# Attention and state-space convolution on one core: the normalization's multiplications go from VectorE to GpSimd, and the order is set anew

## The chip, the core and the metric

The kernel runs on one core of one Trainium2 chip. The metric is device time in microseconds (us) of one execution; each kernel is executed several times and the median is compared. The core has TensorE (PE in the profile, its weight loads PEld), VectorE (DVE), ScalarE (ACT), GpSimd (POOL) and SyncE (SP). SP issues most DMA transfers, GpSimd issues some, among them all those that add into their destination.

## The reference

Two independent layers are computed and laid side by side in the output. The second is attention with 32 query heads that share one key and one value head of 18 numbers:

```python
q = (x @ wq).reshape(B, S, H, Dh).transpose(0, 2, 1, 3)      # S = 2048, H = 32, Dh = 18
k = x @ wk;  v = x @ wv
scores = einsum("bhqd,bkd->bhqk", q, k) * (Dh ** -0.5)
o = einsum("bhqk,bkd->bhqd", softmax(scores, axis=-1), v)
b = o.transpose(0, 2, 1, 3).reshape(B, S, H * Dh) @ wo
```

The first is a long convolution of a 2048 x 576 input along its length, with a kernel that is a sum of 128 complex exponentials per channel, computed by transforms:

```python
P = exp(logdA[:, :, None] * l[None, None, :])                # 576 channels, 128 states, 2048 positions
K = einsum("dn,dnl,dn->dl", Cc, P, dB).real
y = irfft(rfft(pad(u)) * rfft(pad(K)))[:, :L] + u * Dskip
```

## The kernel before

Attention works through four chunks c of 512 queries. In a chunk, 16 pairs of heads run over 16 blocks kb of 128 keys; one such step for two heads is a *score step*, and there are 1024. A score step is two half-precision matmuls on TensorE (tile `s`), one exponential on ScalarE over 128x1024 (tile `P`), and the products of `P` with the values, in full precision, summed in PSUM (tile `ops`). The values have a column of ones, so that each head's sum of exponentials comes out as row 18 of its 32 rows. TensorE gets three score steps at a time; between them it does the products and *filler*: the projections of the queries (`q`), bounds for the exponent (`up`), the output projection (`op`), and the matmuls of the convolution (`kg`, `hu`, `lu`, `hk`, `lk`, `iy`).

`gather` (L768) copies the finished `ops` of four heads to SBUF on VectorE (tile `o`) and stores it to DRAM (`od`). When a chunk's eight groups are stored, `normalize` (L777) makes the rows that the output projection reads:

- it loads the sums (`dn`), takes reciprocals on VectorE and stores them (`rden`),
- it loads the unnormalized rows into `oT`, in five parts m of 126 rows (the last has 72),
- for each part it loads the reciprocals of its heads, each repeated over 18 rows (tile `db`, two buffers), and multiplies `oT` by them.

The first three chunks are normalized whole (15 multiplications). The last is done in four pieces as its head groups finish (`LATE`, 4 multiplications), and what its output projection has not reached by the last exponential is done in `finish` (L822), in matmuls called `fin`.

The convolution runs in 12 blocks beside it. VectorE builds tables (`tab`, `tt`), spectra (`ks` of the kernel, `us` of the input) and their products (`acc`, `t`); GpSimd issues the DMAs that add one tile into another: one `ks<-ks` per block, after whose landing the products `acc<-us,ks` may start, and two `acc<-t` with a `t<-t` between them, after whose landing the block is transformed back. GpSimd also issues the stores of the projected queries (`qd`) and of their bounds (`sd`).

One instruction stream per engine is written out by a planner in the kernel's own code. `Clock` keeps an estimated time for each engine and for each piece of memory, and the parts of the kernel are generators (`Stream`, L384) that yield what they wait for: `"p"` for a turn on TensorE, `"v"` for a time on VectorE's clock. The order in which they are resumed by these estimates is the order in which instructions are written into the engines' queues. On the chip each engine takes its queue strictly in that order and waits on semaphores for its inputs. The filler shares one bank of PSUM (`bank`, L479), so its next matmuls wait for VectorE's copy out of that bank.

In `normalize` the multiplication is written into VectorE's queue when the planner's clock says that `db` and `oT` have landed. The constants that the estimates use (`HOP`, `FETCH`, `SLACK`, `OVER`, `BACK`, `WF`) stand at the top of the file.

Of the kernel before, what the change touches and what calls it, by code (L numbers as in the profile page):

```python
# [13 lines left out]
ALU = mybir.AluOpType  # L14
# [39 lines left out]
URGENT = 9.6825  # L54
HELD = 0
PATIENCE = 0
SLACK = 0.1532
FEW = 9
NEW = 3
LET = -0.0566  # L60
PLAN = 0.7938
START = 11.4238
OVER = 0.8933
CLEAR = 1.826

LATE = {1: [0], 3: [1], 5: [2], 6: [3]}
# [10 lines left out]
HALF_PI = 1.5707963  # L77


HOP = 0.0401  # L80
GRAIN = 128
FIRST = 25.4233
FETCH = 4.0451
ROOM = 0.3903
INTO = 0.114
BACK = 0.0861
TIGHT = 0.1942
WF = 6.8815
WI = 0.9251
WK = 0.9218  # L90
WB = 1.4569
EPS = 0.0224


# [10 lines left out]
class Clock:  # L105
# [15 lines left out]
    def reset(self, t, v, a):  # L121
        self.t, self.v, self.a, self.g, self.q, self.fill = t, v, a, a, a, 0.0
        self.mem = {}
        self.lanes = [[], []]
        self.block, self.since = self.n // 256, t - FETCH

    def fetch(self):

        if self.n // 256 != self.block:
            self.t = max(self.t, self.since + FETCH * (self.n // 256 - self.block))  # L130
            self.block, self.since = self.n // 256, self.t
# [54 lines left out]
    def end(self, e, t, out, ins, lag):  # L186
        for x in ins:
            c = self.cells(x)
            if c:
                c[1][c[3]] = np.maximum(c[1][c[3]], t + HOP)  # L190
        c = self.cells(out) if out is not None else None
# [3 lines left out]
    def turn(self, mode):  # L195

        if mode != self.mode:
            self.t += INTO if mode else BACK
            self.mode = mode

    def pe(self, cost, out=None, ins=()):
        self.fetch()
        self.turn(0)
        self.t = self.begin(1, self.t, out, tuple(ins)) + cost
        self.end(1, self.t, out, tuple(ins), 0.166 + HOP)

    def act(self, cost, out=None, ins=(), func=None):
# [3 lines left out]
        self.a = self.begin(2, self.a, out, ins) + cost  # L211
        self.end(2, self.a, out, ins, 0.12 + HOP)
        return self.a

    def dve(self, cost, out, ins):
        self.v = self.begin(3, self.v, out, ins) + cost
        self.end(3, self.v, out, ins, 0.09 + HOP)
        self.work += cost
# [39 lines left out]
    def land(self, r, t, new):  # L258
        old, r[3] = r[3], t
        for c, k, lag in ((r[4], 0, HOP), (r[5], 1, HOP)):  # L260
            if c and t != old:
# [6 lines left out]
    def filled(self):  # L268

        self.fill = self.v + HOP + 0.03  # L270


class Queue:
# [5 lines left out]
    def dma_start(self, out, src, **k):  # L279
        self.k.dma(self.name, out, src, "accum_op" in k)  # L280
        return self.q.dma_start(out, src, **k)  # L281

    def activation(self, out, src, func, **k):
        self.k.act(0.07 + math.prod(out.shape[1:]) / 1.2e3, out, (src,), func)
        return self.q.activation(out, src, func, **k)
# [29 lines left out]
class Vector:  # L315
# [13 lines left out]
    def tensor_tensor(self, out, a, b, **k):  # L329
        self.cost(1.042e-3, out, a, b)  # L330
        return self.v.tensor_tensor(out, a, b, **k)  # L331
# [26 lines left out]
class Stream:  # L358
# [30 lines left out]
    def go(self, step, credit, lock=None):  # L389
# [4 lines left out]
        if self.kind == "p":  # L394
            ready = self.ready if self.holds else max(self.ready, k.fill)
            if credit <= 0 or k.t < ready - EPS or lock not in (None, self):
                return False
        if self.kind == "v" and (max(k.t, k.v) < self.ready - EPS or k.v > k.t + self.ahead):
            return False
# [16 lines left out]
class Attention:  # L416
# [342 lines left out]
    def normalize(self, c, ms):  # L759

        nc, V, K = self.nc, self.V, self.k
        od = self.od[c].rearrange("(h r) n -> h r n", r=32)
        if ms[0] == 0:
            self.oT = self.cp.tile([P, 5, CT], F32, tag="oT", name=f"oT{c}")
        o = self.oT
        h0, h1 = MT[ms[0]][0] // DH, sum(MT[ms[-1]]) // DH
        n = (h1 - h0) * CT // P
        dn = self.p1.tile([P, P], F32, tag="dn", name=f"dn{c}_{h0}")  # L768
        rd = self.dr.tile([H, CT], F32, tag="rden", name=f"rden{c}_{h0}")
        nc.sync.dma_start(dn[:n, :], od[h0:h1, DH, :].rearrange("h (a n) -> h a n", n=P))  # L770
        yield "v", lambda: K.at(dn), False
        V.tensor_scalar(dn[:n, :], dn[:n, :], 1e-37, None, op0=ALU.max)
        V.reciprocal(dn[:n, :], dn[:n, :])
        nc.sync.dma_start(rd[h0:h1, :].rearrange("h (a n) -> (h a) n", n=P), dn[:n, :])
        for m in ms:
            m0, mn = MT[m]
            nc.sync.dma_start(o[:mn, m, :], od[m0 // DH:(m0 + mn) // DH, 0:DH, :])  # L777
        tiles = {}

        def fetch(m):  # L780
            m0, mn = MT[m]
            tiles[m] = self.p1.tile([P, CT], F32, tag="db", name=f"db{c}_{m}", bufs=2)
            nc.sync.dma_start(tiles[m][:mn, :], rd[m0 // DH:(m0 + mn) // DH, :].unsqueeze(1).broadcast_to([mn // DH, DH, CT]))
        for m in ms[:2]:
            fetch(m)
        for m in ms:
            mn = MT[m][1]
            yield "v", lambda: K.at(tiles[m], o[:, m, :]), False
            V.tensor_tensor(o[:mn, m, :], o[:mn, m, :], tiles[m][:mn, :], op=ALU.mult)
            if m + 2 in ms:  # L790
                fetch(m + 2)

# [177 lines left out]
    def main(self, conv, flag):  # L970
# [29 lines left out]
        def beside(left, new):  # L1000
# [3 lines left out]
            if new and self.due < self.step + URGENT:  # L1004
                left += OVER
            elif new and any(st.live and st.kind == "p" and st.ready < K.t + CLEAR for st in conv.streams):
# [34 lines left out]
        def fill(i):  # L1041

            free = max(K.s[(i + j) % NS] - 0.225 * j for j in range(NS)) - 0.113
            late = free + SLACK
            while True:
# [150 lines left out]
class Conv:  # L1196
# [384 lines left out]
    def early(self):  # L1581
# [5 lines left out]
        self.streams = [Stream(g, self.k) for g in (self.fronts(), self.inputs(), self.kernels(), self.backs())]  # L1587
        for st, share in zip(self.streams, (WF, WI, WK, WB)):
            st.share = share
# [188 lines left out]
```

## Time and profile before

| what | value |
|---|---|
| median of 3 runs | 1154.71 us (1153.86 to 1155.09) |
| the profiled execution's own time | 1157.21 us |
| its span on the core | 1155.0 us |
| granted TensorE clock over the span | 0.992 |
| TensorE busy | 1096.4 us, 95% |
| ScalarE busy | 1021.8 us, 88% |
| VectorE busy | 935.8 us, 81% |
| GpSimd busy | 96.4 us, 8%, nearly all of it the issuing of DMAs |

The share of VectorE is a mean: it is higher in most stages and falls when the convolution ends. In the rows below an instruction's line is L281, L296 or L331 where a helper issues it (a DMA, a matmul, VectorE's tensor_tensor), so the tile names tell which one it is. A number in square brackets behind a row of the timeline is the time for which that engine stood idle before it, and what released it. The row "PEclk" is the share of its clock that TensorE was granted.

### The profile page before, as it was taken

Reading aid. Unit: us, or ns where it says so; the run is one execution under the profiler, and the core shown is the slowest. Engines: PE = TensorE matmul, PEld = TensorE weight load, DVE = VectorE, ACT = ScalarE, POOL = GpSimd, SP = SyncE. Lnnn points to the kernel's source line nnn. Section 1 sums busy time; section 2 is a strip of 40 time slices with the busy share of each in tenths; the row PEclk is TensorE's granted clock in tenths of the full one; section 3 lists DMA queues with packets and bytes.
Section 4 is the critical chain, followed back from the end, with each engine's and each line's share of the span. In section 5 each row is a group of like instructions: output and inputs, shape, how many; then the busy total and the mean of one; then the engine's idle time right before and its main releaser. Section 6 shows DMA issues by size and latency. Waiting matters only on the chain. (4 is left out here: it accounts for less than half of the span.)

```text
span 1155.0 us, 42904 instructions
## 1 busy us (share of the span) xinstructions
PE 1096.4 (95%) x18660; PEld 556.4 (48%) x18660; DVE 935.8 (81%) x1910; ACT 1021.8 (88%) x1092; POOL 96.4 (8%) x150
## 2 busy tenths in 40 slices
PE   7999979999998899999999999999989899999997
PEld 2454544445454455544454455545544445555444
DVE  5988964878797898998988998989999887873423
ACT  4998969999996998999999899999999898989993
POOL 1100110121010000001011100000010200001000
PEclk9999989999998999999999999999999999999999
DMA  7322442244233316127144325144261413235211
GB/s 282 130 64 94 113 112 79 77 112 117 93 92 96 113 46 145 39 72 197 45 148 108 87 67 160 33 122 106 77 164 42 138 58 80 82 68 129 83 39 45
DMA packets 55124, 114.19 MB, mean 99 GB/s; under 512 B 7500, under 2 KB 25053, under 8 KB 53651
## 3 DMA queue, kind: packets, MB, share of 16 engines
q1 hardware_dynamic: 43715, 77.88, 20.3%
q0 software_dynamic: 10784, 33.10, 14.0%
q8 instruction: 148, 2.42, 0.9%
q10 hardware_dynamic: 432, 0.43, 0.1%
q14 instruction: 45, 0.37, 0.1%
HBM read 48.60 MB, written 36.60 MB: 74 GB/s over the span
## 5 line engine op out<-in xcount | busy, mean ns | idle before, releaser
L749 ACT ACTIVATE P<-s 128x1024 f32<-128x1024 f32 x992 | 941.3, 1028 | 96.5 <-PE s L296 89.5
L296 PE MATMUL ops<-P,v_sb 128*32 128x256 f32 (+1 forms) x8848 | 551.6, 367 | 9.3 <-DVE o L335 7.1
L296 PEld LDWEIGHTS ops<-P,v_sb 128*32 128x32 f32 x8848 | 267.9, 110 | 212.5 <-issue 72.2
L296 PE MATMUL s<-aug,kaug 55*128 55x512 f16 x2048 | 294.1, 382 | 9.8 <-ACT P L749 7.4
L296 PEld LDWEIGHTS <-kaug 55*128 55x128 f16 x2048 | 95.6, 94 | 192.2 <-issue 144.1
L296 PE MATMUL q<-x,wq_sb 128*32 128x256 f32 x1360 | 86.0, 383 | 3.2 <-DVE un L343 3.2
L296 PE MATMUL op<-wo_sb,oT 126*32 126x288 f32 (+1 forms) x1096 | 79.3, 408 | 2.1 <-DVE out L335 2.1
L331 DVE TENSOR_TENSOR tab<-tab,tt 128x576 f32<-128x576 f32 (+1 forms) x72 | 59.2, 822 | 1.7
L296 PEld LDWEIGHTS q<-x,wq_sb 128*32 128x32 f32 x1360 | 40.7, 110 | 39.2 <-issue 11.0
L331 DVE TENSOR_TENSOR tab<-tab 128x576 f32<-128x576 f32 (+1 forms) x72 | 58.9, 819 | 0.0
L331 DVE TENSOR_TENSOR ks<-ks 128x384 f32<-128x384 f32 (+2 forms) x84 | 55.8, 669 | 1.4
L331 DVE TENSOR_TENSOR t<-us,ks 128x576 f32<-128x576 f32 x72 | 50.4, 753 | 0.0
L296 PEld LDWEIGHTS op<-wo_sb,oT 126*32 126x32 f32 (+1 forms) x1096 | 33.1, 110 | 31.4 <-issue 6.2
L331 DVE TENSOR_TENSOR acc<-acc 128x768 f32<-128x768 f32 (+1 forms) x48 | 40.5, 855 | 8.1 <-DMA acc<-t 7.5
L281 POOL DMA_DIRECT2D qd<-qh x46 | 25.9, 596 | 220.1 <-DVE qh L339 214.7
L296 PE MATMUL kg<-tab 128*32 128x64 f32 x2304 | 42.3, 220 | 1.6 <-DVE ksb L335 0.4
L296 PEld LDWEIGHTS kg<-tab 128*32 128x32 f32 x2304 | 36.2, 110 | 14.5 <-issue 4.8
L281 POOL DMA_DIRECT2D acc<-t x24 | 20.7, 863 | 254.9 <-PE s L296 66.0
L331 DVE TENSOR_TENSOR us<-us 128x384 f32<-128x384 f32 (+1 forms) x60 | 37.1, 634 | 1.0
L331 DVE TENSOR_TENSOR acc<-us,ks 128x768 f32<-128x768 f32 x36 | 32.6, 953 | 4.6 <-DMA ks<-ks 4.6
L331 DVE TENSOR_TENSOR us<-lu,scu 128x384 f32<-128x384 f32 x48 | 24.4, 550 | 14.3 <-PE lu L296 14.3
L747 ACT ACTIVATE P<-s,nb 128x1024 f32<-128x1024 f32 x32 | 32.9, 1117 | 2.5 <-PE s L296 2.4
(457 smaller groups left out, 1052.5 us busy)
## 6 DMA issues: line engine op xcount, KB each, us to landing
acc<-t POOLq DMA_DIRECT2D x12, 864.0 KB, 7.5
od<-o SPq DMA_DIRECT2D x31, 256.0 KB
park<-two SPq DMA_DIRECT2D x6, 1152.0 KB
acc<-t POOLq DMA_DIRECT2D x12, 576.0 KB, 5.7
aug<-qd SPq DMA_DIRECT2D x124, 54.0 KB
u<-u SPq DMA_DIRECT2D x12, 384.0 KB
kd<-ksb SPq DMA_DIRECT2D x12, 384.0 KB
kt<-kd SPq DMA_DIRECT2D x48, 96.0 KB
```

The source lines that it names most:

```text
L281: return self.q.dma_start(out, src, **k)
L296: return self.e.matmul(out, w, x, **k)
L331: return self.v.tensor_tensor(out, a, b, **k)
L747: nc.scalar.activation(pt, ps, AF.Exp, scale=SCALE / UNIT ** 2, bias=self.nb)
L749: nc.scalar.activation(pt, ps, AF.Exp, scale=SCALE / UNIT ** 2)
```

## The change

The multiplication of `oT` by `db` is issued to GpSimd. It is written into GpSimd's queue right behind the loads of its operands, before the planner's clock has them landed; the planner then books 1.3 us for it on GpSimd's clock (`POOLED`) and resumes the generator when the product should be there. Seven constants of the planner change as well, so the order of all engines' queues is written anew. Arithmetic, tiles and DMA transfers are the same.

```diff
-SLACK = 0.1532
+SLACK = 0.1682
-OVER = 0.8933
+OVER = 0.8763
-HOP = 0.0401
+HOP = 0.0421
-FETCH = 4.0451
+FETCH = 2.983
-BACK = 0.0861
+BACK = 0.0872
-WF = 6.8815
+WF = 6.9146
+POOLED = 1.3
...
+    def tensor_tensor(self, out, a, b, **k):
+        return self.q.tensor_tensor(out, a, b, **k)
...
         for m in ms:
             mn = MT[m][1]
-            yield "v", lambda: K.at(tiles[m], o[:, m, :]), False
-            V.tensor_tensor(o[:mn, m, :], o[:mn, m, :], tiles[m][:mn, :], op=ALU.mult)
+            K.g = K.begin(4, K.g, o[:, m, :], (o[:, m, :], tiles[m])) + POOLED
+            K.end(4, K.g, o[:, m, :], (o[:, m, :], tiles[m]), 0.15)
+            nc.gpsimd.tensor_tensor(o[:mn, m, :], o[:mn, m, :], tiles[m][:mn, :], op=ALU.mult)
+            yield "v", lambda: K.at(o[:, m, :]), False
             if m + 2 in ms:
                 fetch(m + 2)
```

All queues are word for word the same up to score step 129 of 1024; behind it they differ throughout. TensorE has the same work: 36 of its 256-column products are split into two of 128 columns, and 12 matmuls of the last chunk's output projection are named `fin` instead of `op`, which is the third place below.

VectorE, normalization of the first chunk, where it copies a finished `ops` to SBUF (`o_0`). Before:

```order
533 L331 TENSOR_TENSOR tab_1_4911<-sum_4502,r__4418 128x24x32
534 L331 TENSOR_TENSOR tab_1_4911<-r__4418,dif_4503 128x24x32
535 L331 TENSOR_TENSOR tt_1_8_0_5123<-f__4196,sum_4502 128x768
536 L331 TENSOR_TENSOR oT_4679<-oT_4679,db_2_5002 126x512
537 L331 TENSOR_TENSOR oT_4679<-oT_4679,db_3_5024 126x512
538 L335 COPY o_0_5158<-ops_0_4684 128x512
```

and now:

```order
537 L335 TENSOR_TENSOR tab_1_4899<-tab_1_4899 128x24x24
538 L335 TENSOR_TENSOR tab_1_4899<-tab_1_4899,tt_1_8_4_5103 128x24x24
539 L335 TENSOR_TENSOR acc_5176<-us_3756,ks_4522 128x4x4x48 x2
540 L343 TENSOR_SCALAR qh_1_5100<-q_1_0_5141 128x256
541 L355 SCALAR_TENSOR_TENSOR ql_1_5101<-q_1_0_5141,qh_1_5100 128x256
542 L339 COPY o_0_5206<-ops_0_4684 128x512
```

The copy stood behind two multiplications that wait for `db`; now it stands behind products `acc<-us,ks`, whose operand `ks` is completed by a DMA from GpSimd's queue.

GpSimd, the same place. Before:

```order
45 L281 DMA ks_4454<-ks_4454 128x768
46 L281 DMA acc_4947<-t_4948 128x1728
47 L281 DMA qd_5018<-qh_0_4468 128x512 x2
48 L281 DMA qd_5018<-ql_0_4469 128x512
49 L281 DMA sd_5019<-sh_0_5113 56x1x64
50 L281 DMA t_4949<-t_4949 128x576
51 L281 DMA acc_4947<-t_4949 128x1152
```

and now:

```order
45 L285 ISA
46 L285 TENSOR_TENSOR oT_4704<-oT_4704,db_0_4914 126x512
47 L282 DMA qd_5000<-qh_0_4496 128x512 x2
48 L282 DMA qd_5000<-ql_0_4497 128x512
49 L285 TENSOR_TENSOR oT_4704<-oT_4704,db_1_4916 126x512
50 L282 DMA sd_5001<-sh_0_5097 56x1x64
51 L285 TENSOR_TENSOR oT_4704<-oT_4704,db_2_5081 126x512
52 L282 DMA ks_4522<-ks_4522 128x768
53 L285 TENSOR_TENSOR oT_4704<-oT_4704,db_3_5134 126x512
54 L282 DMA acc_5176<-t_5177 128x1728
55 L282 DMA t_5178<-t_5178 128x576
56 L282 DMA acc_5176<-t_5178 128x1152
```

The adding DMAs of the convolution and the stores of the queries now stand behind multiplications that wait for their own loads. A new instruction named ISA stands ahead of the first of them.

TensorE, from the last products to the first reciprocals' broadcast (`bc`), in `finish`. Before:

```order
6695 L296 MATMUL ops_7_16698<-P_14_15_16998,v_sb 32x256 x2
6696 L296 MATMUL ops_7_16698<-P_15_15_17021,v_sb 32x256 x2
6697 L296 MATMUL fin_17039<-wo_sb,oT_16194 32x288 x12
6698 L296 MATMUL fin_17040<-wo_sb,oT_16194 32x288 x8
6699 L296 MATMUL bc<-rc_last,b_16723 32x256 x4
```

and now:

```order
6711 L300 MATMUL ops_7_16716<-P_14_15_17016,v_sb 32x256 x2
6712 L300 MATMUL ops_7_16716<-P_15_15_17039,v_sb 32x256 x2
6713 L300 MATMUL fin_17057<-wo_sb,oT_16416 32x288 x16
6714 L300 MATMUL fin_17058<-wo_sb,oT_16416 32x288 x8
6715 L300 MATMUL bc<-rc_last,b_16774 32x256 x4
```

Four of the 12 matmuls that moved behind the last product stand here, the other eight further down in the same tail: the last chunk's output projection starts nine score steps later (before step 975, now 984) and advances by one part every three steps in both.

## Prediction

> **What bounds the kernel now.** I read the page's busy times first, then the busy times by stage, then the timeline wherever TensorE stood idle.
>
> ```profile
> PE 1096.4 (95%) x18660; PEld 556.4 (48%) x18660; DVE 935.8 (81%) x1910; ACT 1021.8 (88%) x1092; POOL 96.4 (8%) x150
> ...
> core 0: us, PE busy (x) PEld busy (x) DVE busy (x) ACT busy (x) POOL busy (x), PEclk, DMA share, GB/s
> 0.00:168.00 168.00, 152.62 (x2432) 72.24 (x2436) 136.48 (x301) 133.52 (x142) 19.53 (x37) 0.98 0.44 134
> 347.00:352.00 5.00, 0.61 (x12) 0.13 (x4) 2.11 (x4) 2.13 (x3) 0.00 (x0) 0.94 0.30 108
> 352.00:358.00 6.00, 5.75 (x54) 2.46 (x58) 4.69 (x8) 2.75 (x3) 1.39 (x2) 0.50 0.50 124
> 366.00:620.00 254.00, 244.38 (x4375) 126.89 (x4375) 230.13 (x482) 235.45 (x254) 19.28 (x29) 1.00 0.36 101
> 890.00:915.00 25.00, 20.55 (x354) 9.62 (x350) 21.61 (x47) 19.95 (x22) 4.81 (x9) 1.00 0.29 93
> 1070.00:1135.00 65.00, 62.99 (x876) 29.76 (x876) 20.40 (x40) 62.05 (x67) 0.00 (x0) 1.00 0.15 51
> ```
>
> TensorE bounds the run until about 1070 us: its work is the same after the change, so time can only come from its 58.6 us without work (1155.0 less 1096.4), or from a lower clock. From 1070 to 1135 ScalarE is nearest to full (62.05 of 65) and the convolution is over. TensorE's worst stage is 347 to 352, with 0.61 us of work in 5; right behind it the granted clock is 0.50 for 6 us, where 54 matmuls took 5.75 us. At full clock that is half, so the slow clock costs another 2.9 us. VectorE is 90% busy from 366 to 620 (230.13 of 254): a wait in its queue is not made up soon.
>
> The timeline of 347 to 352 shows why TensorE had nothing (VectorE's rows, then TensorE's):
>
> ```profile
> 346.38 0.94 DVE L331 TENSOR_TENSOR tt<-f__4196,sum 128x768 f32<-128x768 f32 x1
> 349.54 0.69 DVE L331 TENSOR_TENSOR oT<-oT,db 126x512 f32<-126x512 f32 x1 [2.22 <-DMA db<-rden]
> 350.90 0.69 DVE L331 TENSOR_TENSOR oT<-oT,db 126x512 f32<-126x512 f32 x1 [0.67 <-DMA db<-rden]
> 351.51 0.68 DVE L335 COPY o<-ops 128x512 f32<-128x512 f32 x1
> ...
> 352.25 2.36 PE L296 MATMUL ops<-P,v_sb 128*32 128x256 f32 x24 [4.64 <-DVE o L335]
> ```
>
> The copy that frees TensorE's PSUM bank needs no `db`, but stands behind two multiplications that do. The same happens twice more:
>
> ```profile
> 652.52 0.69 DVE L331 TENSOR_TENSOR oT<-oT,db 72x512 f32<-72x512 f32 x1 [1.19 <-DMA db<-rden]
> 653.13 1.01 DVE L331 TENSOR_TENSOR us<-lu,scu 128x384 f32<-128x384 f32 x2
> 654.29 0.86 PE L296 MATMUL hu<-u,dft_sb 128*32 128x192 f32 x16 [1.14 <-DVE us L331]
> ...
> 904.96 0.69 DVE L331 TENSOR_TENSOR oT<-oT,db 126x512 f32<-126x512 f32 x1 [2.05 <-DMA db<-rden]
> 905.57 0.16 DVE L343 TENSOR_REDUCE un<-up 128x1 f32<-128x8 f32 x1
> 905.79 1.50 PE L296 MATMUL q<-x,wq_sb 128*32 128x256 f32 x24 [2.93 <-DVE un L343]
> ```
>
> **The change, part by part.** *Removed from VectorE:* 19 multiplications and their waits.
>
> ```profile
> L331 DVE TENSOR_TENSOR oT<-oT,db 126x512 f32<-126x512 f32 (+1 forms) x19 | 12.9, 689 | 12.0 <-DMA db<-rden 12.0
> ```
>
> That is 12.9 us of work and 12.0 us of waiting. VectorE is not the bound, so I count only what TensorE lost by it: 4.64 + 1.14 + 2.93 = 8.71 us, and 2.9 us by the slow clock that followed the longest. Together **-11.6 us**. The other multiplications stood where TensorE had work, and count nothing.
>
> *Added on GpSimd:* 19 multiplications, of which no row here shows one. From below each takes 0.69 us as on VectorE; from above I use the slowest elementwise instruction per column:
>
> ```profile
> 1137.12 1.75 DVE L877 RECIPROCAL rc_last<-rc_last 128x256 f32<-128x256 f32 x1
> L281 POOL DMA_DIRECT2D ks<-ks x12 | 10.8, 900 | 277.5 <-DVE ksb L335 155.6 <-DVE ks L331 73.9 <-DVE raw L331 31.2
> ks<-ks POOLq DMA_DIRECT2D x12, 384.0 KB, 4.4
> ```
>
> Twice 1.75 is 3.5 us for 512 columns. I take twice VectorE's, 1.4 us, nearer to the lower row since a product is one simple operation per element. GpSimd is 8% busy, so 19 x 1.4 = 27 us fit; what counts is who stands behind. The ISA instruction ahead of the first one has no duration here; the queue is idle ahead of it (277.5 us of waiting before the `ks` DMAs alone), so I cost it at nothing, and at the time the first multiplication would be late if that cover is gone.
>
> The Trainium skill (GPSIMD Engine Reference, section 3.1) gives some 2.6 cycles per element at 1.2 GHz for an operation with two inputs. Estimated from that page, 512 columns take 1.1 us and a little for dispatch; the sum would be the same.
>
> *Turned into a new wait:* the multiplication is queued before its loads have landed, so GpSimd's queue stands still until they have. How long a load takes:
>
> ```profile
> 329.69 0.34 SPq L281 DMA_DIRECT2D rden<-dn  x1
> 333.16 0.78 SPq L281 DMA_DIRECT2D db<-rden  x1
> 337.84 0.69 DVE L331 TENSOR_TENSOR oT<-oT,db 126x512 f32<-126x512 f32 x1 [0.39 <-DMA db<-rden]
> 338.56 0.73 SPq L281 DMA_DIRECT2D db<-rden  x1
> ```
>
> From the reciprocals' store (329.69) to the first multiplication (337.84) are 8.2 us; the third `db`, issued at 338.56, was used at 349.54, 11 us later, in a stage with a large `acc<-t` in flight. Behind these waits stand now (GpSimd's order, above) the stores of the queries, which are needed a chunk later and cost nothing, and the adding DMAs. In the first chunk `ks<-ks` waits for the third multiplication. From the reciprocals I add 8.2 us to the first, 1.4 for it, 4.7 for the next `db` (333.16 to 337.84), 1.4 for the third and 4.4 for `ks` to land: about 20 us. VectorE's product that reads `ks` was written some 18 score steps behind the first `db` load, and at the pace of the row from 366 to 620 (254 exponentials, one per step, in 254 us) that is 18 us; at the 1.1 us per step of the whole run (1155/1024) it is 20. So it comes out even, with nothing to spare, and three rows behind it stands the copy that TensorE waits for. What such a wait costs at worst, the first block shows:
>
> ```profile
> 154.93 1.83 DVE L331 TENSOR_TENSOR acc<-acc 128x768 f32<-128x768 f32 x2 [5.53 <-DMA acc<-t]
> ...
> 161.40 1.51 PE L296 MATMUL iy<-acc,dft_sb 128*32 128x192 f32 x16 [5.79 <-issue]
> ```
>
> The bounds for each of three chunks are 0 and 5.79 us plus a slow clock. I take 2.2 us in all, the longest lateness of a `db` seen above, once: **+2.2 us**. (That row's stall lies at step 126, where the order is unchanged, and stays.)
>
> *Moved into the tail:* 12 matmuls, 24 in the profile's count, which shows each full-precision one as two.
>
> ```profile
> 1139.66 4.86 PE fin L296 x80
> ```
>
> At 4.86/80 each, 24 take **+1.5 us**, on a chain that is TensorE's alone. What they leave behind lies under ScalarE's exponentials (62.05 of 65) and gives nothing back.
>
> *Written anew:* the other waits behind step 129. The largest of them, all for VectorE:
>
> ```profile
> 213.69 0.28 PE L296 MATMUL up<-aw,all 128*32 128x8 f32 x13 [2.46 <-DVE aw L339]
> 401.14 1.66 PE L296 MATMUL op<-wo_sb,oT 126*32 126x288 f32 x24 [2.10 <-DVE out L335]
> 541.13 0.86 PE L296 MATMUL lu<-u,dft_sb 128*32 128x192 f32 x16 [2.04 <-DVE scu L335]
> 855.55 0.86 PE L296 MATMUL hu<-u,dft_sb 128*32 128x192 f32 x16 [1.86 <-DVE us L331]
> ```
>
> They sum to 8.46 us. A new order can lose these and make others; I take 0, with -8.5 and +8.5 as bounds. The 36 split products keep their columns: 0.
>
> Sum: -11.6 + 2.2 + 1.5 = **-7.9 us**. The profiled execution took 1157.21 us (2.21 beside its span), 2.50 above the median; I apply the difference to both: 1149.3 for a profiled execution, **1146.8 us** for the median.
>
> **The rivals.**
>
> *Larger gain.* VectorE, freed of 25 us, is also earlier at the waits just shown. For it: all four are for VectorE in stages where it is 90% busy. Against: none lies near a multiplication. Half of them is -4.2: 1142.6 us.
>
> *The gain is eaten: VectorE stands while GpSimd multiplies.* If two engines reading the same memory hold each other up, each of the 15 multiplications beside the convolution costs VectorE 1.4 us instead of 0.69: 15 x 0.7 = 10.5 us in a queue that is 90% full. If TensorE pays all of it, the sum is +2.6, 1157.3; if half, 1152.1 us. For it: three waits of 1 to 2 us on VectorE were enough for 8.7 us on TensorE. Against: the copies out of PSUM are not two-input reads, and no row here shows GpSimd holding VectorE up, as it computes nothing. The Trainium skill (SBUF — State Buffer, "SBUF: two separate sides") speaks against this change: a VectorE instruction with two SBUF inputs and a GpSimd instruction that reads SBUF take a shared port exclusively, for the whole instruction. By that rule, this is what happens.
>
> *Slower: GpSimd's queue holds the convolution back.* The place is a `ks<-ks` or `acc<-t` behind a multiplication; it decides once a multiplication ends later than VectorE reaches the product behind it. For it: the even count above, and loads that took 11 us. Against: the `acc<-t` that slowed that load now stands behind it. At the first block's price, 5.79 + 2.9 = 8.7 us, one such chunk gives -1.4 in all (the 2.2 replaced), still no slower; two give -11.6 + 17.4 + 1.5 = +7.3: 1162.0 us.
>
> **How the numbers follow.** A run of this kernel can tell about 0.2% (2.3 us) from no change. Chances: the forecast 0.46, larger gain 0.14, eaten 0.18, slower 0.22. The first two are faster by more than 0.2% (0.60), the third is within it (0.18), the fourth slower (0.22). The likeliest's own range is 1142 to 1151. The range for 8 in 10 goes from 1139 (all four waits gone, 1146.8 - 8.5 = 1138.3) to 1162 (the slower case).
>
> **What would show it right or wrong.** Right: no VectorE row waits for `db`; TensorE's three stalls at the copy, `us` and `un` are gone and the clock stays at 1.00 beyond 218 us; the stall at 155.6 us stays; the tail behind the last exponential is 1.5 us longer; GpSimd's multiplications take 0.7 to 3.5 us, near 1.4. Wrong: VectorE's two-input rows become longer while GpSimd multiplies (eaten); VectorE rows `acc<-us,ks` or `acc<-acc` wait for `ks` or `acc` by several us in the three normalizations, with TensorE idle behind (slower); or the idle time of TensorE outside them differs by more than 8.5 us, which the removed waits don't explain.

## The result, and the profile after

The changed kernel takes 1172.85 us (median of 5 runs, 1171.47 to 1176.92) beside 1153.86 us for the kernel before (5 runs, 1152.53 to 1155.09): 1.017 of its time, 95% interval 1.0151 to 1.0189. It is slower by 1.7%, about 19.6 us, where 7.9 us faster (1146.8 us) was forecast, and lies above the range of 1139 to 1162 us. The profiled execution took 1176.92 us, the longest of the five, its span 1175.1, and the granted clock over the span was 0.986 (0.992 before).

From the page of the changed kernel, the busy times and three of the groups (busy time, mean ns of one, idle time before them and what ended it):

```profile
PE 1106.2 (94%) x18732; PEld 560.6 (48%) x18732; DVE 941.9 (80%) x1888; ACT 1022.4 (87%) x1092; POOL 124.2 (11%) x169
...
L335 DVE TENSOR_TENSOR acc<-us,ks 128x768 f32<-128x768 f32 x36 | 34.6, 995 | 13.4 <-DMA ks<-ks 13.4
...
L285 POOL TENSOR_TENSOR oT<-oT,db 126x512 f32<-126x512 f32 (+1 forms) x19 | 28.6, 1546 | 131.2 <-DMA db<-rden 93.2
```

Two things are to be seen. TensorE's time without work rose from 58.6 to 68.9 us (1175.1 less 1106.2), and its busy time rose by 9.8 us for the same products. And VectorE, which lost 12.9 us of multiplications, is busy 6.1 us *longer* than before, 941.9 for 935.8. So some 19 us were added to instructions that it already had.

The timeline shows where. This is the first normalization of the changed kernel (VectorE, GpSimd, and TensorE's next wait):

```profile
337.55 1.53 POOL L285 TENSOR_TENSOR oT<-oT,db 126x512 f32<-126x512 f32 x1 [40.20 <-DMA db<-rden]
337.85 2.05 DVE L335 TENSOR_TENSOR tt<-f__4140,sum 128x768 f32<-128x768 f32 x1
339.83 3.02 DVE L335 TENSOR_TENSOR tab<-tab 128x768 f32<-128x768 f32 x1
340.73 1.28 POOL L285 TENSOR_TENSOR oT<-oT,db 126x512 f32<-126x512 f32 x1
342.88 0.96 DVE L335 TENSOR_TENSOR tab<-tab,tt 128x768 f32<-128x768 f32 x1
343.75 0.16 DVE L347 TENSOR_REDUCE un<-up 128x1 f32<-128x8 f32 x1
343.96 3.19 PE L300 MATMUL q<-x,wq_sb 128*32 128x256 f32 x32 [2.62 <-DVE un L347]
...
345.26 2.87 POOL L285 TENSOR_TENSOR oT<-oT,db 126x512 f32<-126x512 f32 x1
345.59 0.74 DVE L335 TENSOR_TENSOR tt<-f__4140,sum 128x576 f32<-128x576 f32 x1
```

Products of 128x768 take 0.95 us, as the row at 342.88 does. The one that meets the multiplication at 337.55 takes 2.05, the one at 340.73 takes 3.02: both end 0.8 us after GpSimd is done. The small reduction that TensorE needs stands behind them, and TensorE waits 2.62 us. Behind that its clock is halved for 3.4 us (below). At 345.26 it is the other way round: GpSimd's multiplication takes 2.87 us, more than twice its 1.28, while VectorE's products beside it keep their usual length (0.74 us). The second normalization (VectorE, GpSimd, TensorE):

```profile
630.59 3.35 DVE L335 TENSOR_TENSOR t<-r__9359,w 128x384 f32<-128x384 f32 x1
630.98 2.53 POOL L285 TENSOR_TENSOR oT<-oT,db 126x512 f32<-126x512 f32 x2
633.87 0.55 DVE L335 TENSOR_TENSOR t<-f__8899,w 128x384 f32<-128x384 f32 x1
...
662.76 1.02 DVE L335 TENSOR_TENSOR us<-lu,scu 128x384 f32<-128x384 f32 x2
662.88 2.84 POOL L285 TENSOR_TENSOR oT<-oT,db 126x512 f32<-126x512 f32 x2
663.70 2.84 DVE L335 TENSOR_TENSOR tab<-r__9359,dif 128x768 f32<-128x768 f32 x1
...
668.93 1.08 PE L300 MATMUL ops<-P,v_sb 128*32 128x256 f32 x8 [2.56 <-DVE o L339]
```

Where two multiplications stand back to back, one product waits for both: 3.35 us for 0.55. The two `us<-lu,scu` at 662.76 take their usual 0.51 each beside GpSimd; one of their operands (`lu`) lies in PSUM. So a VectorE product with both operands in SBUF and a GpSimd multiplication in SBUF do not run together in these rows, one of the two stands; a product with an operand in PSUM does run beside it. The Trainium skill (SBUF — State Buffer, "SBUF: two separate sides") states just this, an exclusive lock on a shared port; the trace agrees (3.35 us for 0.55, and 0.51 for 0.51).

The stalls and the clock. Stretches of the changed kernel, with the granted clock in the column PEclk:

```profile
core 0: us, PE busy (x) PEld busy (x) DVE busy (x) ACT busy (x) POOL busy (x), PEclk, DMA share, GB/s
344.48:347.90 3.42, 3.42 (x32) 1.25 (x26) 3.39 (x5) 0.10 (x1) 3.26 (x2) 0.50 0.25 79
668.75:672.16 3.41, 3.23 (x34) 1.42 (x36) 3.41 (x7) 0.00 (x0) 0.00 (x0) 0.50 0.26 96
```

Between 150 and 1150 us the trace of before has three such stretches of half clock (17.1 us together), that of the changed kernel eight (30.7 us). The 13.6 us more cost about half, 6.8 us of TensorE's 9.8 us longer busy time (an estimate from the half clock).

### The profile page after: what moved, and what is told of

Read it like the earlier page. It is cut to its first block, busy times and chain, and to the rows that moved or that the text cites. A ratio compares the mean times of both kernels' runs of the same rounds, so it can differ in the third digit from the quotient of the medians.

```text
span 1175.1 us, 43064 instructions
## 1 busy us (share of the span) xinstructions
PE 1106.2 (94%) x18732; PEld 560.6 (48%) x18732; DVE 941.9 (80%) x1888; ACT 1022.4 (87%) x1092; POOL 124.2 (11%) x169
## 5 line engine op out<-in xcount | busy, mean ns | idle before, releaser
L300 PE MATMUL ops<-P,v_sb 128*32 128x256 f32 (+1 forms) x8920 | 554.6, 366 | 12.9 <-DVE o L339 7.2
L300 PE MATMUL op<-wo_sb,oT 126*32 126x288 f32 (+1 forms) x1072 | 76.8, 408 | 2.4 <-DVE ob L339 1.4
L335 DVE TENSOR_TENSOR acc<-acc 128x768 f32<-128x768 f32 (+1 forms) x48 | 41.5, 874 | 18.5 <-DMA acc<-t 17.8
L335 DVE TENSOR_TENSOR acc<-us,ks 128x768 f32<-128x768 f32 x36 | 34.6, 995 | 13.4 <-DMA ks<-ks 13.4
L285 POOL TENSOR_TENSOR oT<-oT,db 126x512 f32<-126x512 f32 (+1 forms) x19 | 28.6, 1546 | 131.2 <-DMA db<-rden 93.2
L282 POOL DMA_DIRECT2D ks<-ks x12 | 10.7, 894 | 299.6 <-DVE ksb L339 144.0
L335 DVE TENSOR_TENSOR us<-us 128x384 f32<-128x384 f32 (+1 forms) x60 | 40.0, 682 | 1.0
```

The source lines that it names most:

```text
L285: return self.q.tensor_tensor(out, a, b, **k)
L300: return self.e.matmul(out, w, x, **k)
```

## The experiments

Three causes could have made the loss, and each would show in its own way. *The hold:* VectorE stands while GpSimd multiplies. *The order:* the newly written order is worse for itself, whoever multiplies. *The queue:* the adding DMAs and stores stand behind multiplications that wait for their loads. (The expectations call them theory L, O and Q.) All ratios are to the kernel before, timed beside each kernel on the same chip (its medians were 1152.5 to 1153.0 us); 1% is 11.5 us.

### Separating the order from the multiplications

**The order of before, GpSimd multiplies.** The planner is told that VectorE still has the multiplication, so every queue keeps its order; only the engine changes.

```diff
-            V.tensor_tensor(o[:mn, m, :], o[:mn, m, :], tiles[m][:mn, :], op=ALU.mult)
+            V.cost(1.042e-3, o[:mn, m, :], o[:mn, m, :], tiles[m][:mn, :])
+            nc.nc.gpsimd.tensor_tensor(o[:mn, m, :], o[:mn, m, :], tiles[m][:mn, :], op=ALU.mult)
```

> The order of before, unchanged row for row on every engine, but the 19 multiplications are issued to GpSimd at the place in the program where VectorE had them. Theory L (VectorE's two-input instructions are held while GpSimd multiplies): the three stalls of before go (-11.6 us), but each of the 15 multiplications beside the convolution holds VectorE for about 1.2 us, and TensorE pays 8 to 15 us of that: 1150 to 1160 us, with VectorE rows of 2 to 3 us beside GpSimd's. Theory O (the new order alone is slow): no holding matters, 1142 us. Theory Q (GpSimd's queue delays ks and acc): here a multiplication is queued only when its loads should have landed, so 1142 to 1147 us.

Measured: 0.9967 (0.9951 to 0.9983), 1149.74 us. Faster than before, by 0.3%. VectorE and GpSimd in this run, at the place of the 4.64 us stall:

```profile
337.52 2.92 DVE L331 TENSOR_TENSOR t<-us,ks 128x576 f32<-128x576 f32 x1
338.51 1.32 POOL L790 TENSOR_TENSOR oT<-oT,db 126x512 f32<-126x512 f32 x1
...
344.93 0.67 DVE L335 COPY o<-ops 128x512 f32<-128x512 f32 x1
...
347.78 1.28 POOL L790 TENSOR_TENSOR oT<-oT,db 126x512 f32<-126x512 f32 x1 [4.46 <-DMA db<-rden]
347.85 2.02 DVE L331 TENSOR_TENSOR tab<-tab,tt 128x768 f32<-128x768 f32 x1
```

The copy `o` no longer waits for `db` and TensorE's stall is gone; GpSimd waits in its place (4.46 us). That is not free: `t<-t` stands behind it in GpSimd's queue and goes out at 352.29, 6 us after its input was made (346.27), and at 362 us VectorE waits 2.21 us for the `acc` that follows from it, and TensorE 1.33. The hold is there as well: 2.92 us for a product of 0.75.

**The order's constants alone.** Six constants of the change (the seventh, POOLED, is for GpSimd's multiplication), VectorE multiplies.

```diff
-SLACK = 0.1532
+SLACK = 0.1682
...
-WF = 6.8815
+WF = 6.9146
```

> The kernel before with the six changed constants of the planner, the multiplications on VectorE as before: the order set anew without the move. Theory L: about that of before, 1148 to 1160 us. Theory O: as slow as the change, 1168 to 1174 us. Theory Q: as L.

Measured: 1.0112 (1.0076 to 1.0147), 1164.45 us. The constants alone cost more than half of the loss. This order is not the changed kernel's own, since the planner also reckons with who multiplies, so the next pair matters more.

**No multiplication, in both orders.** GpSimd waits for the same loads, copies one column and writes ones over the tile, so that it reads next to nothing; that VectorE is then not held, the rows below show. The normalization is left out. Once in the changed kernel, once in the order of before.

```diff
-            nc.gpsimd.tensor_tensor(o[:mn, m, :], o[:mn, m, :], tiles[m][:mn, :], op=ALU.mult)
+            nc.nc.gpsimd.tensor_copy(o[:mn, m, 0:1], tiles[m][:mn, 0:1])
+            nc.nc.gpsimd.memset(o[:mn, m, :], 1.0)
```

> The changed kernel with its order, but GpSimd does not multiply: in the place of each multiplication it copies one column of the loaded reciprocals into the tile (so that it still waits for the load) and then fills the tile with ones, a write that reads nothing. The normalization is left out, so the attention half of the output is not the reference's. Theory L: nothing holds VectorE, the stalls of 2.62, 1.62, 2.56, 2.09 and 1.32 us beside held rows go, and three stretches of half clock with them (10.2 + 5.1 us): 1155 to 1160 us. Theory O and theory Q: 1168 to 1173 us, since order and waits in GpSimd's queue stay.

> The order of before, with the multiplications replaced on GpSimd by the one-column copy and the fill (normalization left out, as in the run before). All theories: VectorE neither waits nor is held, so this is what taking the multiplications off VectorE is worth at best: 11.6 us, 1142 to 1144 us. If it stays at 1150 or above, the three stalls of before were not worth what I counted.

Measured: 1.0019 (1.0000 to 1.0038), 1154.87 us in the changed order; 0.9916 (0.9889 to 0.9943), 1142.67 us in the order of before. This pair divides the loss:

| step | from ratios | us |
|---|---|---|
| VectorE freed of multiplications and their waits | 0.9916 - 1 | -9.7 (±3.1) |
| the new order, nobody multiplies | 1.0019 - 0.9916 | +11.9 (±3.8) |
| GpSimd multiplies, in the new order | 1.017 - 1.0019 | +17.4 (±3.1) |
| sum | 1.017 - 1 | +19.6 |
| GpSimd multiplies, in the order of before | 0.9967 - 0.9916 | +5.9 (±3.6) |

VectorE's groups show the hold directly. The changed kernel, shapes apart:

```profile
L335 DVE TENSOR_TENSOR acc<-acc 128x768 f32<-128x768 f32 x36 | 34.8, 979 | 18.1 <-DMA acc<-t 17.8
...
L335 DVE TENSOR_TENSOR tab<-tab 128x768 f32<-128x768 f32 x24 | 24.9, 1036 | 0.0
L335 DVE TENSOR_TENSOR us<-lu,scu 128x384 f32<-128x384 f32 x48 | 24.4, 551 | 12.4 <-PE lu L300 12.4
...
L335 DVE TENSOR_TENSOR us<-us 128x768 f32<-128x768 f32 x12 | 14.3, 1195 | 0.1
```

and the same order without the multiplication:

```profile
L335 DVE TENSOR_TENSOR acc<-acc 128x768 f32<-128x768 f32 x36 | 33.8, 951 | 19.2 <-DMA acc<-t 19.0
L335 DVE TENSOR_TENSOR acc<-us,ks 128x768 f32<-128x768 f32 x36 | 33.0, 952 | 12.5 <-DMA ks<-ks 12.5
L335 DVE TENSOR_TENSOR us<-lu,scu 128x384 f32<-128x384 f32 x48 | 24.4, 549 | 11.4 <-PE lu L300 11.4
L335 DVE TENSOR_TENSOR tab<-tab 128x768 f32<-128x768 f32 x24 | 22.8, 948 | 0.0
...
L335 DVE TENSOR_TENSOR us<-us 128x768 f32<-128x768 f32 x12 | 11.4, 953 | 0.1
```

`us<-us` falls from 1195 to 953 ns and `tab<-tab` from 1036 to 948, the means that they had before; `us<-lu,scu`, with its operand in PSUM, is the same in both. The waits for `acc` and `ks` (19.0 and 12.5 us, beside 7.5 and 4.6 in the kernel before) stay. So the multiplying doesn't make them; whether GpSimd's queue does is asked below.

What the order costs lies mostly behind step 800. Both of the next rows, busy times in a stretch with nobody multiplying, reach about from score step 810 to step 957 (the second begins and ends two to three steps earlier). In the changed order:

```profile
905.00:1065.00 160.00, 151.95 (x2646) 78.73 (x2642) 122.31 (x221) 140.64 (x148) 12.81 (x18) 1.00 0.37 89
```

and in the order of before:

```profile
905.00:1057.00 152.00, 151.29 (x2661) 78.86 (x2656) 111.54 (x202) 139.54 (x148) 11.65 (x15) 1.00 0.37 91
```

TensorE's work is the same, 152 and 151 us. Counted by the starts of the exponentials, the 147 steps take 160.4 us for 152.0; the steps from 129 to 810 take 736.0 for 737.5, so up to there the new order lost nothing. VectorE has 122.31 us of work in the stretch for 111.54: in the new order more of the last blocks is left for this end. TensorE is idle in it for 8.05 us against 0.71, and three waits for VectorE make most of that (new order, nobody multiplying):

```profile
910.04 0.87 PE L300 MATMUL hk<-kt,dft_sb 128*32 128x192 f32 x16 [2.02 <-DVE ksb L339]
1004.84 0.86 PE L300 MATMUL hu<-u,dft_sb 128*32 128x192 f32 x16 [1.87 <-DVE ob L339]
1064.57 0.86 PE L300 MATMUL iy<-acc,dft_sb 128*32 128x192 f32 x16 [2.90 <-DVE acc L335]
```

The split products are longer work. TensorE's groups of the kernel before:

```profile
L296 PE MATMUL ops<-P,v_sb 128*32 128x256 f32 x7536 | 511.2, 383 | 8.5 <-DVE o L335 6.2 <-ACT P L749 1.0 <-issue 0.6
...
L296 PE MATMUL ops<-P,v_sb 128*32 128x128 f32 x1312 | 67.2, 276 | 0.8 <-DVE o L335 0.8
```

In the changed order with nobody multiplying it is 507.7 us for 7464 and 74.6 for 1456. Together that is 578.4 us before and 582.3 now, 3.9 more for the same columns. By the rows of the kernel before, two products of 128 take 34.6 ns longer than one of 256, 2.5 us for all 72; the rest was not followed. Two thirds of the splits lie before step 800, where the new order lost nothing, so it is not shown that they are a part of the 11.9 us.

### Is it the queue?

**The changed kernel without the waits for `db` and without the hold.** As above, but only the ones are written, so GpSimd does not wait for `db` (it still waits for the loads of `oT`, over which it writes).

```diff
-            nc.gpsimd.tensor_tensor(o[:mn, m, :], o[:mn, m, :], tiles[m][:mn, :], op=ALU.mult)
+            nc.nc.gpsimd.memset(o[:mn, m, :], 1.0)
```

> The changed kernel's order with the fill alone in the place of each multiplication: GpSimd neither reads nor waits for the reciprocals' load (normalization left out). Against the run with the one-column copy (1154.9) this takes the wait out of GpSimd's queue. Theory Q: ks, acc and t are issued earlier, 1149 to 1153 us. If the queue's waits are covered, as the copy's run suggests: 1153 to 1157 us.

Measured: 1.0043 (1.0024 to 1.0063), 1157.05 us, beside 1.0019 with the waits. Taking GpSimd's waits for `db` away (93.2 us in the page of the changed kernel) gained nothing; 58.6 us of waits for `oT` are left in this run. VectorE's waits for `acc` and `ks` are as long as in the changed kernel (17.8 and 13.7 us here, 17.8 and 13.4 there). And they don't stand where GpSimd's queue is held up. In the changed kernel:

```profile
929.41 1.41 POOL L285 TENSOR_TENSOR oT<-oT,db 72x512 f32<-72x512 f32 x1 [0.62 <-DMA db<-rden]
1018.30 0.96 DVE L335 TENSOR_TENSOR acc<-us,ks 128x768 f32<-128x768 f32 x1 [4.61 <-DMA ks<-ks]
1079.11 0.96 DVE L335 TENSOR_TENSOR acc<-acc 128x768 f32<-128x768 f32 x1 [10.95 <-DMA acc<-t]
1109.66 1.28 POOL L285 TENSOR_TENSOR oT<-oT,db 126x512 f32<-126x512 f32 x1 [37.91 <-PE s L300]
```

These are the two longest such waits behind step 129. The DMAs that they wait for were issued between the two multiplications shown, and no other multiplication stands between them. In the three normalizations themselves the longest wait for `ks` or `acc` is 1.24 us (at 925.36). So in the changed kernel the queue is not the cause; the two longest waits belong to the late convolution. In the order of before the queue does cost something, in the one place named above (and once more below).

### How the hold's price goes with its length

**Doubled.** The order of before; behind each multiplication a second of the same size (into the tile of the reciprocals, whose next load therefore waits for it too).

```diff
+            nc.nc.gpsimd.tensor_tensor(tiles[m][:mn, :], o[:mn, m, :], tiles[m][:mn, :], op=ALU.mult)
```

> The first of these runs (order of before, multiplications on GpSimd) with a second multiplication of the same size behind each, into the tile of reciprocals that is no longer needed. Theory L: the cost of holding, 7 us there (1149.7 against 1142.7 without any multiplication), doubles or more, since two behind each other hold VectorE in one piece: 1156 to 1162 us, with VectorE rows of 3 to 4 us. Theory Q (only what stands behind in GpSimd's queue counts): 1.3 us more for that queue, 1150 to 1152 us.

Measured: 1.0094 (1.0061 to 1.0126), 1163.63 us.

**In four pieces**, in the order of before and in the changed kernel.

```diff
+            for f in range(4):
+                w = slice(f * HN, f * HN + HN)
+                nc.nc.gpsimd.tensor_tensor(o[:mn, m, w], o[:mn, m, w], tiles[m][:mn, w], op=ALU.mult)
```

> The same run as the first with each GpSimd multiplication cut into four of 128 columns; order otherwise unchanged. Theory L with a hold for the length of one instruction: VectorE gets in between the pieces, no row is longer than its own time plus some 0.5 us, and the time lies below the 1149.7 us, 1144 to 1148 us. If GpSimd and VectorE merely share a rate, or GpSimd keeps VectorE out over all four pieces: 1149 to 1153 us, rows of 2 us and more as before.

> The changed kernel, its order unchanged, with each GpSimd multiplication cut into four of 128 columns. In the order of before this gained nothing over whole ones (1150.3 against 1149.7). In the changed order multiplications pile up behind each other and hold VectorE for up to 3.9 us in one row. If the length of one hold is what TensorE cannot hide: 18 us become 7 or less, 1157 to 1164 us. If only the sum of the holds counts: 1168 to 1174 us, as the change.

Measured: 0.9969 (0.9953 to 0.9984), 1150.32 us in the order of before, as with whole multiplications; 1.0132 (1.0106 to 1.0157), 1166.42 us in the changed kernel, by the ratios 4.4 us (±3.7) less than with whole ones. The timeline of the first (order of before) has both faces of the hold:

```profile
347.46 5.22 POOL L792 TENSOR_TENSOR oT<-oT,db 126x128 f32<-126x128 f32 x7 [5.80 <-DMA db<-rden]
347.71 1.02 DVE L331 TENSOR_TENSOR tab<-r__4418,dif 128x576 f32<-128x576 f32 x1
...
644.52 3.63 POOL L792 TENSOR_TENSOR oT<-oT,db 126x128 f32<-126x128 f32 x8
644.61 1.02 DVE L331 TENSOR_TENSOR us<-lu,scu 128x384 f32<-128x384 f32 x2 [0.22 <-PE lu L296]
645.55 3.23 DVE L331 TENSOR_TENSOR tab<-tab,tt 128x576 f32<-128x576 f32 x1
```

At 347 the engines take turns: a product of 0.75 us takes 1.02, held for one piece at most, and GpSimd's pieces become longer instead (5.22 us for seven). At 644, with eight pieces queued and VectorE busy out of PSUM as they begin, they run through at 0.45 each, and the next product waits for all that are left: 3.23 us. All runs together, VectorE's busy time from each page, held being what it is above the run of the same order without the multiplication:

| order | GpSimd does | VectorE busy | held | ratio | us lost to the hold |
|---|---|---|---|---|---|
| of before | nothing long | 924.3 | 0 | 0.9916 | 0 |
| of before | four pieces each | 932.2 | 7.9 | 0.9969 | 6.1 |
| of before | one each | 935.2 | 10.9 | 0.9967 | 5.9 |
| of before | two each | 945.4 | 21.1 | 1.0094 | 20.5 |
| new | nothing long | 923.0 | 0 | 1.0019 | 0 |
| new | four pieces each | 934.4 | 11.4 | 1.0132 | 13.0 |
| new | one each (the change) | 941.9 | 18.9 | 1.0170 | 17.4 |

The last column is uncertain by 3 to 5 us in each row. In the new order a microsecond of VectorE held costs about one of run time (13.0 for 11.4, 17.4 for 18.9); in the order of before half of one at 10.9, and nearly all at 21.1. The half may be too little: the run without multiplications, from which it is counted, carries a stall of 3.84 us that GpSimd's queue makes, with a half clock behind it (shown further down), the run with whole ones only 1.33 us of it. That is some 4 us (an estimate: 3.84 + 1.7 - 1.33). That the pieces keep GpSimd busy longer (144.7 for 124.2 us in the changed order) and yet save time speaks against the queue a second time.

### What were the old waits worth?

**Wait without work.** The order of before; VectorE multiplies one column instead of 512, so its waits for `db` stay and its work goes (the other columns are not normalized).

```diff
-            V.tensor_tensor(o[:mn, m, :], o[:mn, m, :], tiles[m][:mn, :], op=ALU.mult)
+            V.cost(1.042e-3, o[:mn, m, :], o[:mn, m, :], tiles[m][:mn, :])
+            V.v.tensor_tensor(o[:mn, m, 0:1], o[:mn, m, 0:1], tiles[m][:mn, 0:1], op=ALU.mult)
```

> The order of before on all engines, but VectorE multiplies one column of each part alone (the rest of the normalization is left out): its waits for db stay, 12.9 us of work become about 1.5. Leaving out both was worth 10 us. If the waits were worth it, as predicted: 1150 to 1154 us. If it was the work, in a queue that is 90% full: 1142 to 1147 us.

Measured: 0.9969 (0.9954 to 0.9985), 1148.63 us. The work alone is worth 3.6 us (±1.8), the waits the other 6.1 (0.9969 - 0.9916, ±3.6), net of the stall that GpSimd's queue makes in the run without multiplications (shown further down). The stall is still there in this run (VectorE, then TensorE):

```profile
346.54 0.16 DVE L790 TENSOR_TENSOR oT<-oT,db 126x1 f32<-126x1 f32 x1 [2.64 <-DMA db<-rden]
...
348.14 0.69 DVE L335 COPY o<-ops 128x512 f32<-128x512 f32 x1
...
348.89 1.51 PE L296 MATMUL ops<-P,v_sb 128*32 128x256 f32 x12 [4.18 <-DVE o L335]
```

**The multiplications moved on.** VectorE multiplies, TensorE's order is that of before, but the last three multiplications of each of the first three chunks stand seven VectorE instructions later, so that `db` has more time to land; the load of the fifth `db` goes with the third. The same kernel was timed twice.

```diff
+DEFER = 7
...
+            def late(m=m, mn=mn):
+                V.v.tensor_tensor(o[:mn, m, :], o[:mn, m, :], tiles[m][:mn, :], op=ALU.mult)
...
+            K.pending.append([DEFER if m > 1 else 0, late])
```

> The order of before on TensorE, row for row, and the multiplications on VectorE; only the third to fifth multiplication of the first three chunks stand seven VectorE operations later (and the load of the fifth part's reciprocals behind the third of them), so that the copy, us and un that TensorE waited for stand ahead of them. If TensorE's three stalls come from what stands behind these waits, they go without any holding: the 8.7 us and the slow clock of 2.9, as in the run without multiplications (1142.7): 1141 to 1146 us. If the waits merely move to whatever stands behind the multiplications now: 1149 to 1154 us.

> The run with the third to fifth multiplication moved on (1150.6), again, for its profile, which was disturbed. Its gain was 2.4 us, where 11.6 were expected. If the waits moved to what stands behind the multiplications: VectorE rows of oT with waits of 1 to 4 us and TensorE idle behind each. If the three stalls are gone and others take their place elsewhere: no such rows, and TensorE idle where it was busy before.

Measured: 0.9978 (0.9964 to 0.9993), 1150.61 us, and again 0.999 (0.997 to 1.001), 1151.96 us: a gain of 0.2 and 0.1%, the second within the noise. The stall at 348 us is gone, but in the second run VectorE waits 2.08 us for the fifth `db` at 650.5, and TensorE stands 2.67 us before `hk` and 3.56 before `up` at 903. Moved by hand to this one place, the waits come up elsewhere; other places were not tried.

### Is it one of the constants?

With nothing else changed, each of these writes another order, VectorE multiplying as before:

```diff
-FETCH = 4.0451
+FETCH = 2.983
```

> The kernel before with only FETCH = 2.983, multiplications on VectorE. All six constants together cost 12 us. If the lower FETCH lets the planner put work closer together than the chip can take it: 1160 to 1166 us. If any change of the constants gives an order of its own, with stalls of its own: anywhere from 1150 to 1166, and another set of large TensorE waits.

```diff
-            yield "v", lambda: K.at(tiles[m], o[:, m, :]), False
+            yield "v", lambda: K.at(tiles[m], o[:, m, :]) + 1.5, False
```

> The kernel before with the multiplications on VectorE, but the planner takes their loads to land 1.5 us later, so that they are written into VectorE's queue later; the order behind changes with that. If the three stalls of before come from loads that land later than the planner thinks, VectorE's waits for db fall from 12 us to under 4 and the time by up to 11 us: 1143 to 1150 us. If the new order costs as much as it did with the other constants: 1153 to 1163 us.

```diff
-HOP = 0.0401
+HOP = 0.0421
```

> The kernel before with only HOP = 0.0421, 2 ns more for each handover between engines in the planner, multiplications on VectorE. No reason for a gain or a loss lies in the 2 ns themselves. If the constants' values matter (FETCH above all): 1151 to 1156 us, as before. If any new order loses against the one of before, whose constants were fitted to it: 1157 to 1167 us.

```diff
-WF = 6.8815
+WF = 6.9146
```

> The kernel before with only WF = 6.9146 (the share of turns that the convolution's tables get, up by 0.5%), multiplications on VectorE. As the run before: 1151 to 1156 us if the values matter, 1157 to 1167 us if any new order loses.

And the changed code with the constants of before (GpSimd multiplies, `POOLED` stays):

```diff
-SLACK = 0.1682
+SLACK = 0.1532
...
-WF = 6.9146
+WF = 6.8815
```

> The changed code with the planner's constants of before: multiplications on GpSimd, queued before their loads have landed, and an order that only the changed code sets anew. Theory L: holding costs 7 to 18 us, the waits removed give back 10 to 12: 1150 to 1162 us. If the six constants are what makes the new order slow: at least 10 us below the changed kernel's 1172.9. If every new order costs about 12: 1160 to 1173 us.

Measured, none of the five without loss (the last has GpSimd multiply, so its loss holds the hold's price too):

| order written with | ratio | 95% interval |
|---|---|---|
| `db` due 1.5 us later | 1.0067 | 1.0045 to 1.0089 |
| FETCH alone | 1.0121 | 1.0076 to 1.0165 |
| HOP alone | 1.0195 | 1.0156 to 1.0234 |
| WF alone | 1.0349 | 1.0323 to 1.0375 |
| changed code, constants of before | 1.0169 | 1.0144 to 1.0193 |

It is no one constant's doing: with all six as before, the changed code loses as much as with the new ones. SLACK, OVER and BACK were not set alone. Each of the six orders written anew with no GpSimd multiplication lost between 0.7 and 3.5% against that of before, the change's own among them (1.0%). Why each does was not followed, nor why the order of before is the best of them; for the change's own it is the late convolution shown above.

The fastest kernel that computes everything is that of the first experiment, the order of before with GpSimd multiplying (in four pieces it is the same): 0.9967 of before, 0.980 of the changed kernel (0.9967/1.017).

## Why the prediction was wrong, step by step

The miss is 27.5 us, from -7.9 to +19.6. The hold, which the sum left out, is 17.4 of them; the new order, 11.9 for the 3.7 of the sum (+2.2, +1.5 and 0), is 8.2; the removed waits, -9.7 for -11.6, are 1.9.

- **Removed from VectorE (-11.6).** Near by the number, partly by luck: -9.7 us (±3.1). In the order of before the three stalls went as said, but the waits alone are worth some 6.1 of it, and "count nothing" for the multiplications' own work was wrong (3.6 us). In the changed kernel two stalls came back through the hold, before `un` (2.62 us) and behind the copy (2.56, above). And in the order of before with nobody multiplying a new one took something away (VectorE, GpSimd, TensorE):

```profile
343.25 0.74 DVE L331 TENSOR_TENSOR t<-us,ks 128x576 f32<-128x576 f32 x1
348.32 0.71 POOL L790 COPY oT<-db 126x1 f32<-126x1 f32 x1 [2.37 <-DMA db<-rden]
349.62 0.91 POOL L281 DMA_DIRECT2D t<-t  x1
362.76 0.96 DVE L331 TENSOR_TENSOR acc<-acc 128x768 f32<-128x768 f32 x1 [4.71 <-DMA acc<-t]
...
364.04 1.51 PE L296 MATMUL kg<-tab 128*32 128x64 f32 x48 [3.84 <-DVE ksb L335]
```

  The input of `t<-t` is made at 343.99, but GpSimd stands before it, waiting 3.99 and 2.37 us for two `db`, and issues it at 349.62, 5.6 us later; in the kernel before it went out 0.3 us after its input. The `acc<-t` behind it is late by that, VectorE waits 4.71 us and TensorE 3.84, and a stretch of 3.4 us at half clock begins there. This is the wait in GpSimd's queue that the prediction priced, in an order that the change does not have.
- **A multiplication on GpSimd at 1.4 us.** Right: 1.28 alone, 1.55 on average with the waits for VectorE in it. The ISA instruction cost nothing that shows: the first multiplication waited for its `db` (row at 337.55). The Trainium skill's rate (GPSIMD Engine Reference, section 3.1) gave an estimate of 1.1; measured is 1.28.
- **The new wait in GpSimd's queue (+2.2), and the slower rival (+7.3).** Wrong for the changed kernel: nothing (1.0043 without the waits for `db`, 1.0019 with them). VectorE does wait longer for `ks` and `acc`, but not in the three normalizations, where the sign was to be looked for, and as long with GpSimd's waits for `db` taken away. The mechanism itself is real, as the rows just shown say.
- **The tail (+1.5).** From the scores of the last step to the end it takes 21.9 us for 21.0: +0.9.
- **Written anew (0, with ±8.5), and the split products (0).** This is one of the two steps that failed. The new order costs 11.9 us (±3.8) by itself, 11.0 without the tail, where 0 was taken and 8.5 was the bound. What the runs show in its place is VectorE late with the convolution behind step 810, and TensorE waiting for it in three places (2.02, 1.87 and 2.90 us). The bound was made from the waits that could be seen before; an order can make new ones that are in no trace yet, and the 72 split products of the profile's count, put at 0 as well (+3.9 us of TensorE's work), could have been priced from two groups of the page: 67.8 ns for a product of 256 columns (511.2/7536) and twice 51.2 for two of 128 (67.2/1312) give +2.5.
- **"The gain is eaten".** This rival, given 0.18, was what happened, and leaving it out of the sum is the other step that failed, and the larger one. Its size was off as well: the price was 15 x (1.4 - 0.69) = 10.5 us, with the 0.69 that VectorE saves already taken off. But the removed work had been costed at nothing in the first term, so the hold is due in full: VectorE was held 18.9 us, and TensorE paid 17.4 of them. What the prediction held against it, that the copies out of PSUM are not two-input reads, is true of the copies and did not help: they stand in VectorE's queue behind the products that are held (2.56 us before `ops`, above).
- **The signs.** Right: no VectorE row waits for `db`; the early stall stays (5.85 for 5.79 us). Wrong: the clock does not stay at 1.00 beyond 218 us, it is halved in six stretches behind that; the longer two-input rows, the sign of the eaten gain, are there.

## What to carry to other kernels

Before work goes to GpSimd beside a busy VectorE, count which VectorE instructions beside it work on SBUF alone, those with two inputs there above all: each meeting can cost VectorE the whole GpSimd instruction (here 12.9 us of work left it, and 18.9 us of standing came, for 15 multiplications of 1.28 us). When a change lets a planner write its order anew, time the change in the old order (0.9967 here) and the new order without the change (1.0112 with the constants alone): here the order cost 11.9 us, and one constant moved by 0.5% cost 3.5%. When a wait moves to another engine, look at what stands behind it in that engine's queue: a stall removed is worth what is left after the next wait comes up.

## What was not expected of the hardware

- **The hold is longer than the multiplication.** The product at 339.83 is held although GpSimd's row starts only at 340.73, 0.90 us later, and ends 0.83 us after it: 3.02 us for 0.95 of work, 2.1 us lost to 1.28. GpSimd's rows are rough, so whether the hold begins before its row does stays open.
- **Not only products with two inputs stand.** The small TENSOR_SCALAR `sh<-u`, which reads one tile, took 1.20 us at 895.54 in the first experiment, beside a multiplication from 895.43 to 896.70, for its usual 0.18.
- **A waiting product is not always let in between two multiplications.** The one at 630.59 stood through two, another at 645.55 through the rest of eight pieces, while at 347 the engines took turns. What decides was not settled. The Trainium skill (SBUF — State Buffer, "SBUF: two separate sides") has the port go to whichever starts first, for the whole of that instruction; the rows at 630.59 (the changed kernel) and 645.55 (four pieces, order of before) show a product that waits through more than one.
- **Short stalls of TensorE cost clock.** Between 200 and 1140 us of the changed kernel stalls of 2.06 to 3.32 us were followed by 3.4 us at half clock in seven cases out of eight (one of 2.39 us was not); in the kernel before in one of four of 2.04 to 2.93 us. In the first experiment such a stretch began at 903.55 with no longer stall than 1.12 us just before it. So length alone does not decide it. In the prediction only the longest stall, 4.64 us, was given such a price. The Trainium skill (TensorE: Matmul & The Clock Gate, Part 1) puts the drop at an idle window of about 3.4 us; here 2.06 us was enough, and 2.93 us once was not.
- **The order's sensitivity** (the planner's, not the chip's). HOP, 5% larger and nothing else, made the kernel 2.0% slower; WF, 0.5% larger, 3.5%.
